# Two background streams of a mixer taken by turns, and its remaining rows loaded by six transfers

## The chip, the cores and the metric

One core of a Trainium2 chip runs the whole program in one launch. The metric is the device time of one execution in microseconds (us). The engines are named as in the profile: PE (TensorE matmuls), PEld (its weight loads), DVE (VectorE), ACT (ScalarE), POOL (GpSimd) and SP (SyncE, which issues most transfers).

## The reference, cut to what is computed

Three layers follow each other on 4 sequences of 576 rows and 512 columns.

```python
# attention, 8 heads of 64: keep the scores within tau of the row's maximum, softmax, times v
x = attn_out.transpose(0, 2, 1, 3).reshape(4, 576, 512)
# token-shift layer: x_prev is x moved by one row
k = np.maximum(xk @ w_k, 0.0); v = k * k @ w_v      # 512 -> 1024 -> 512
r = 1.0 / (1.0 + np.exp(-(xr @ w_r))); x = r * v
# mixer
X = np.fft.fft(np.fft.fft(x, axis=1), axis=2)
u = x + np.real(X)
un = (u - mean(u)) / np.sqrt(var(u) + 1e-6)
out = u + np.maximum(un @ w_ch1, 0.0) @ w_ch2       # 512 -> 2048 -> 512
```

## The kernel before

The program has two parts that overlap at their border. Attention and the token-shift layer (`ffn_stream`) fill the first 613 us. The mixer follows, and it is what the change touches.

**Products by halves.** A float32 matrix product is made of three products of rounded parts (high by high, high by low, low by high). So each weight has to be split into a high and a low part before use. `weight_pieces` (L46) does it in pieces of 256 columns: a load of 256 KB issued by ACT (L56), three DVE operations that put the raw bits together (L69 to L71), a copy on ACT (L75) and a subtraction (L79), which is on DVE for the first two quarters. The mixer's weights are prepared in four quarters; `quarter(q)` (L924) yields 16 times, once for each piece, first the eight of `w_ch1`, then the eight of `w_ch2`. The second quarter, `quarter(1)`, goes into tiles named cB.

**The transform.** The Fourier transform of one batch is made of matrix products with tables, after rows and columns were folded by symmetry. `fft_fold(b)` (L850) loads 256 pairs of rows (`load_pairs`, L753: four transfers of 256 KB) and the remaining rows (`load_rem`, L761), and folds them on DVE and ACT. `load_rem` fills two tiles of 98 rows, `ra` and `rb`: rows 0 to 31, 33 to 64 and 65 to 96 all hold the same 32 rows of the DRAM tensor `xd`, and rows 32 and 97 hold its row 576. That takes six transfers of 64 KB and four of 2 KB a batch, all from SP. `ra` and `rb` lie in the pool tag "o", which has four buffers in all; the tiles `un` of the normalisation (L977) and the last outputs `xnat` of the token-shift layer use the same four. `fft_one(b)` (L870) multiplies by the first tables (PE lines L802 to L805; L805 is the remaining rows' matmul) and `fft_two(b)` (L890) by the second (L817 to L828), and makes u. `fft_fold`, `fft_one` and `fft_two` yield 6, 3 and 2 times.

**The mixer's matmuls.** `mixer` (L1114) goes through pairs (quarter q, groups of 256 rows g). For each of four blocks f it issues `ch1` (L1088 to L1090, tile c1ps) of this pair and `ch2` (L1110 to L1112, tile c2ps) of the pair before. The first pairs are (0,0) to (0,3), then (1,0) to (1,3), then (0,4) and on. `norm(g)` (L975) loads the rows u of a group, normalises them and `turn(g)` (L998) transposes them on PE (L1005) and splits them (L1008 on ACT, L1009 on DVE) into the tile ut that `ch1` reads. `norm(2)` is asked for while (0,0) runs, for use in (0,2).

**The background.** What runs beside the mixer is a generator, `behind` (L1213): the second quarter's pieces, then the transforms of the third batch (b = 2) and the fourth (b = 3). In the first four pairs two steps of it are taken for each f. A scheduler then orders the instructions of every engine by when it expects them to be ready, with the order of the program as priority. So a step's place in the program is a priority, and not a place in time.

```python
behind = chain(
    quarter(1), fft_fold(2), fft_one(2), fft_two(2),
    fft_fold(3), fft_one(3), fft_two(3), fft_last(), done(),
)
```

Of the kernel before, what the change touches and what calls it, by code (L numbers as in the profile page):

```python
# [20 lines left out]
D, FF, FC = 512, 1024, 2048  # L21
# [8 lines left out]
def tile_kernel(ctx: ExitStack, tc: tile.TileContext, a):  # L30
    nc = tc.nc
    pe, dve, act, pool, sp = nc.tensor, nc.vector, nc.scalar, nc.gpsimd, nc.sync
# [5 lines left out]
    xd = [dram.tile([S + 1, D], F32, name=f"xd{b}") for b in range(B)]  # L38
# [45 lines left out]
    def whole(pair, base=0):  # L84
        return lambda c, n: [x[:, c - base:c - base + n] for x in pair]
# [6 lines left out]
    def big(slot, name):  # L92
        return wA.tile([128, 4096], F32R, tag=slot, name=name)

    def halves(p, name):
        return [wA.tile([128, 2048], F32R, tag=f"A{p}{i}", name=f"{name}{p}{i}") for i in range(2)]
# [40 lines left out]
    def settle():  # L137
        go, second[:] = list(second), []
        for f in go:
            f()  # L140
        while pending:
            pending.pop(0)()
# [610 lines left out]
    def load_pairs(b):  # L753
        xa = fp.tile([128, 2, D], F32, tag="xa", name="xa")
        xb = fp.tile([128, 2, D], F32, tag="xb", name="xb")
        for i in range(2):
            sp.dma_start(xa[:, i], xd[b][128 * i:128 * i + 128, :])
            sp.dma_start(xb[:, i], xd[b][288 + 128 * i:416 + 128 * i, :])
        return [(xa[:, i], xb[:, i]) for i in range(2)]

    def load_rem(b):  # L761

        xa = chp.tile([128, D], F32, tag="o", bufs=4, name="ra")[:98]
        xb = chp.tile([128, D], F32, tag="o", bufs=4, name="rb")[:98]
        for r in (0, 33, 65):
            sp.dma_start(xa[r:r + 32], xd[b][256:288, :])
            sp.dma_start(xb[r:r + 32], xd[b][544:576, :])
        for r in (32, 97):
            sp.dma_start(xa[r:r + 1], xd[b][576:577, :])
            sp.dma_start(xb[r:r + 1], xd[b][576:577, :])  # L770
        return xa, xb

    def folded(xa, xb, n):

        p, q, y = (fp.tile([128, 257], F32, tag="w", bufs=5, name=nm) for nm in ("fp", "fq", "fy"))
        act.activation(p[:n, 0:257:256], xa[:, 0:257:256], AF.Copy)
        act.activation(q[:n, 0:257:256], xb[:, 0:257:256], AF.Copy)
        dve.tensor_tensor(p[:n, 1:256], xa[:, 1:256], xb[:, 511:256:-1], op=ALU.add)
        dve.tensor_tensor(q[:n, 1:256], xb[:, 1:256], xa[:, 511:256:-1], op=ALU.add)
        dve.tensor_tensor(y[:n], p[:n], q[:n], op=ALU.add)  # L780
        dve.tensor_tensor(p[:n, 0:256], p[:n, 0:256], q[:n, 0:256], op=ALU.subtract)
        return y, p[:, 0:256]

    def split_tile(x, w, tag):
        hi = fp1.tile([128, w], F32R, tag=tag + "h", bufs=2, name=tag + "h")
        lo = fp1.tile([128, w], F32R, tag=tag + "l", bufs=2, name=tag + "l")
        act.activation(hi, x, AF.Copy)
        dve.tensor_tensor(lo, x, hi.bitcast(F32), op=ALU.subtract)
        return hi, lo

    def stack_tile(x, w, tag):
        st = fp1.tile([98, w], F32R, tag=tag, bufs=1, name=tag)
        act.activation(st, x[:98], AF.Copy)
        dve.tensor_tensor(st[0:33], x[0:33], st[0:33].bitcast(F32), op=ALU.subtract)
        return st
# [12 lines left out]
    def fsplit(hi, lo, ps):  # L808
        act.activation(hi, ps, AF.Copy)
        dve.tensor_tensor(lo, ps, hi.bitcast(F32), op=ALU.subtract)  # L810
# [39 lines left out]
    def fft_fold(b):  # L850
        while written[b] < 2:
            yield
        settle()
        prs = prs_of[b] = load_pairs(b)
        ra, rb = load_rem(b)
        parts_e, parts_o = [], []
        for xa, xb in prs:
            e, o = folded(xa, xb, 128)
            yield
            parts_e.append(split_tile(e, 257, "fse"))  # L860
            parts_o.append(split_tile(o, 256, "fso"))
            yield
        e, o = folded(ra, rb, 98)
        yield
        ske = stack_tile(e, 257, "ske")
        sko = stack_tile(o, 256, "sko")
        fold_of[b] = (parts_e, parts_o, ske, sko)
        yield

    def fft_one(b):  # L870
        parts_e, parts_o, ske, sko = fold_of.pop(b)
        G = [fp.tile([128, 2, 290], F32R, tag=f"G{i}", bufs=1, name=f"G{i}") for i in range(2)]
        Hh = [fp.tile([128, 2, HS], F32R, tag=f"H{i}", bufs=1, name=f"H{i}") for i in range(2)]
        for mc in range(2):
            o = stage_1(parts_e, ske, tc1, tc1r, 290, 128 * mc, 128 * mc + 128)
            fsplit(G[0][:, mc], G[1][:, mc], o)
            o = stage_1(parts_o, sko, ts1, ts1r, HS, 128 * mc, 128 * mc + 128)
            fsplit(Hh[0][:, mc], Hh[1][:, mc], o)
            yield
        o = stage_1(parts_e, ske, tc1, tc1r, 290, 256, 257)  # L880
        fsplit(g1[0:1], g1[32:33], o)
        sl = slice(32 * b, 32 * b + 32)
        act.activation(g1[64:65, sl], o[:, 256:288], AF.Copy)
        dve.tensor_tensor(g1[96:97, sl], o[:, 256:288], g1[0:1, 256:288].bitcast(F32), op=ALU.subtract)
        for i, x in enumerate((G[0], G[1], Hh[0], Hh[1])):
            act.activation(grem[i][:, :, b, :], x[:, :, 256:288].bitcast(F32), AF.Copy)
        spec[b] = (G, Hh)
        yield

    def fft_two(b):  # L890
        G, Hh = spec.pop(b)
        prs = prs_of.pop(b)
        z, _ = stage_2(G, None, 0, 288, 289)
        zr = fp.tile([1, 257], F32, name="zr")
        act.activation(zr, z[0:1, 0:257], AF.Copy)
        for i in range(2):
            pa, pb = stage_2(G, Hh, 0, 128 * i, 128 * i + 128)
            make_u(2 * b + i, pa, pb, *prs[i], z=zr if i == 0 else None)
            yield
# [12 lines left out]
    def chain(*gens):  # L912
        for g in gens:
            yield from g


    wq = {}
    SEVEN = (3,)
# [5 lines left out]
    def quarter(q):  # L924

        if q % 2:
            t = [big(f"B{i}", f"cB{i}") for i in range(2)]
            wq[q] = [[x[:, 2048 * k:2048 * k + 2048] for x in t] for k in range(2)]
        else:
            wq[q] = [halves(0, "cA"), None]  # L930
        todo = []
        for k, src in enumerate(("w_ch1", "w_ch2")):
            def to(c, n, k=k):
                if wq[q][k] is None:
                    wq[q][k] = halves(k, "cA")
                return whole(wq[q][k], 2048 * q)(c, n)

            todo += [(a[src], to, 8 * q + j) for j in ((0, 2, 4, 6, 1, 3, 5, 7) if k == 0 else range(8))]
        if q not in SEVEN:
            yield from weight_pieces(todo, None, stage2, 256, rb=3, bb=2, lows=dve if q < 2 else None)  # L940
            return
        more[q] = xwp.tile([128, 2, 3, 2, 256], F32R, name=f"more{q}")
        todo = todo[:8] + [(s, to if i % 4 != 1 else lambda c, n: None, 8 * q + i)
                           for (s, to, _), i in zip(todo[8:], (0, 1, 3, 2, 4, 5, 7, 6))]
        kept = {}

        def less(x, y, to):
            t = spare(F32)
            dve.tensor_tensor(t, x, y, op=ALU.subtract)
            act.activation(to[0], t, AF.Copy)  # L950
            pool.tensor_tensor(to[1], t, to[0].bitcast(F32), op=ALU.subtract)
            return t

        def then(k, wf):
            p, i = divmod(k - 8, 4)
            if k < 8:
                return
            ext = [[more[q][:, p, m, t] for t in range(2)] for m in range(3)]
            if i == 0:
                kept["b11"] = wf  # L960
            elif i == 1:
                kept["b12"] = wf
                kept["t1"] = less(wf, kept["b11"], whole(wq[q][1])(1024 * p + 256, 256))
            elif i == 2:
                less(wf, kept["b12"], ext[1])
                kept["t2"] = less(wf, kept["t1"], ext[0])
            else:
                less(wf, kept["t2"], ext[2])

        yield from weight_pieces(todo, None, stage2, 256, rb=3, bb=2, then=then)  # L970
# [240 lines left out]
    for _ in cgen:  # L1211
        pass
    behind = chain(  # L1213
        quarter(1), fft_fold(2), fft_one(2), fft_two(2),
        fft_fold(3), fft_one(3), fft_two(3), fft_last(), done(),
    )

# [2 lines left out]
    for (q, gs), f in mixer():  # L1220
        g = gs[-1]
# [142 lines left out]
```

## Time and profile before

| | us |
|---|---|
| median of three runs | 1053.23 |
| lowest and highest | 1051.57, 1055.49 |
| the profiled execution | 1055.04 |
| its span on the core | 1053.0 |
| PE busy in the span | 1003.0 |
| DVE, ACT, POOL busy | 717.3, 536.3, 395.4 |

The span is what the trace covers; some 2.0 us of the profiled execution lie around it. Times in the trace count from the span's start. "PE busy" is the share of time in which a matmul ran, and "PEclk" the clock that PE was granted, as a share of its full 2.4 GHz. A time behind an arrow is idle time of an engine just before an instruction, put down to what came last.

### The profile page before, as it was taken

How to read it: one execution, taken by the hardware profiler on the slowest of the kernel's cores; microseconds unless marked ns; L12 is line 12 of the kernel's file. 1: busy time of each engine (PE TensorE's matmuls, PEld its weight loads, DVE VectorE, ACT ScalarE, POOL GpSimd, SP SyncE). 2: the span in 40 equal slices, each digit the busy share in tenths (PEclk: the TensorE clock that was granted, in tenths of full speed). 3: DMA queues.
4: the chain of work that ended last, by engine and by line, in shares of the span. 5: the costliest groups of instructions: out<-in, count | busy, mean ns of one | idle time of the engine just before them, and what ended most of it. 6: DMA issues, size and time to landing. Idle time of an engine off the chain costs nothing.

```text
span 1053.0 us, 18827 instructions
## 1 busy us (share of the span) xinstructions
PE 1003.0 (95%) x6807; PEld 884.1 (84%) x6807; DVE 717.3 (68%) x1880; ACT 536.3 (51%) x1211; POOL 395.4 (38%) x495
## 2 busy tenths in 40 slices
PE   6887779999999999999999989999999999999998
PEld 4565659988889888999889879898998888889997
DVE  6799988667776685865356889457537449236776
ACT  4688777675866766857265745243313113113332
POOL 1445868465584564844233100000014125112231
PEclk9899989999999999999999989999999999999999
DMA  6442332121211212100613666536325335223221
GB/s 228 146 133 80 118 108 60 48 67 43 72 60 48 73 31 88 51 24 14 198 55 110 202 204 200 159 127 207 119 92 180 130 119 175 96 101 120 101 100 61
DMA packets 45636, 114.52 MB, mean 109 GB/s; under 512 B 6319, under 2 KB 6740, under 8 KB 45544
## 3 DMA queue, kind: packets, MB, share of 16 engines
q1 hardware_dynamic: 27920, 74.47, 22.2%
q10 hardware_dynamic: 12344, 22.13, 6.8%
q0 software_dynamic: 5280, 16.72, 4.4%
q8 instruction: 54, 0.88, 0.4%
q14 instruction: 38, 0.31, 0.1%
HBM read 84.98 MB, written 28.32 MB: 108 GB/s over the span
## 4 chain that ended last, share of the span: by engine, by line
PE 74%; DVE 10%; DMA 6%; ACT 3%; issue 3%; POOL 2%; SPq 0%; ACTq 0%; DVEq 0%; POOLq 0%
PE c1ps L1090 7%; PE c1ps L1089 6%; PE c1ps L1088 6%; PE s L227 5%; PE av L388 5%; PE c2ps L1112 5%; PE c2ps L1110 5%; PE c2ps L1111 5%; PE p L1045 4%; PE t L329 4%; PE kps L408 2%; PE kps L409 2%; PE kps L410 2%; DMA rawqk<-in_qk 2%; PE vps L530 2%
## 5 line engine op out<-in xcount | busy, mean ns | idle before, releaser
L267 DVE TENSOR_REDUCE small<-s 128x1 f32<-128x576 f32 x144 | 106.9, 752 | 48.1 <-PE s L227 37.3
L1159 POOL DMA_DIRECT2D ud<-u x54 | 29.5, 546 | 264.2 <-DVE u L1158 206.3
L290 POOL TENSOR_SCALAR e<-e,small 128x576 f32<-128x576 f32 x112 | 90.1, 811 | 87.9 <-DVE small L637 73.5
L282 DVE SCALAR_TENSOR_TENSOR e<-s,small,e 128x576 f32<-128x576 f32 x128 | 102.7, 812 | 25.6 <-ACT e L278 22.4
L278 ACT ACTIVATE e<-s,small 128x576 f32<-128x576 f32 x128 | 93.9, 745 | 31.1 <-DVE small L267 27.9
L1100 ACT ACTIVATE hh<-c1ps 128x256 fp32r<-128x256 f32 (+1 forms) x84 | 37.1, 443 | 137.2 <-PE c1ps L1090 111.6
L1101 DVE SCALAR_TENSOR_TENSOR hh<-c1ps,hh 128x256 fp32r<-128x256 f32 (+1 forms) x84 | 41.6, 496 | 89.2 <-ACT hh L1100 89.2
L329 PE MATMUL t<-ident,e 128*128 128x128 f32 x512 | 82.5, 278 | 12.9 <-ACT pt L332 6.5
L332 ACT ACTIVATE pt<-t 128x512 f32<-128x512 f32 x128 | 75.2, 599 | 22.3 <-PE t L329 20.6
L329 PEld LDWEIGHTS t<-ident,e 128*128 128x128 f32 x512 | 61.2, 142 | 24.3 <-issue 6.9
L488 POOL TENSOR_TENSOR k<-relu,k 128x288 fp32r<-128x288 f32 x64 | 54.3, 851 | 68.1 <-ACT k L486 63.9
L408 PE MATMUL kps<-xh,wk 128*128 128x288 f32 x256 | 78.1, 306 | 1.7 <-DVE tg L537 0.9
L530 PE MATMUL vps<-k,wv 128*128 128x288 f32 x256 | 77.5, 304 | 0.4 <-ACT tg L518 0.4
L531 PE MATMUL vps<-k,wv 128*128 128x288 f32 x256 | 77.3, 303 | 0.0
L532 PE MATMUL vps<-k,wv 128*128 128x288 f32 x256 | 76.7, 301 | 0.0
L410 PE MATMUL kps<-xh,wk 128*128 128x288 f32 x256 | 76.2, 298 | 0.0
L409 PE MATMUL kps<-xl,wk 128*128 128x288 f32 x256 | 76.2, 298 | 0.0
L1090 PE MATMUL c1ps<-ut,cB 128*128 128x256 f32 (+1 forms) x256 | 76.0, 297 | 0.0
L1089 PE MATMUL c1ps<-ut,cB 128*128 128x256 f32 (+1 forms) x256 | 75.8, 296 | 0.0
L1088 PE MATMUL c1ps<-ut,cB 128*128 128x256 f32 (+1 forms) x256 | 75.7, 296 | 0.0
L1088 PE MATMUL c1ps<-ut,cA 128*128 128x256 f32 (+1 forms) x224 | 71.0, 317 | 1.4 <-ACT ut L1008 1.4
L1089 PE MATMUL c1ps<-ut,cA 128*128 128x256 f32 (+1 forms) x224 | 70.7, 316 | 0.0
(270 smaller groups left out, 3116.4 us busy)
## 6 DMA issues: line engine op xcount, KB each, us to landing
u<-ud SPq DMA_DIRECT2D x36, 512.0 KB
wraw<-in_w_ch ACTq DMA_DIRECT2D x64, 256.0 KB
rawqk<-in_qk SPq DMA_DIRECT2D x24, 608.0 KB
ud<-u POOLq DMA_DIRECT2D x54, 256.0 KB, 2.5
v<-in_v SPq DMA_DIRECT2D x16, 320.0 KB
un<-ud SPq DMA_DIRECT2D x18, 256.0 KB
out<-u SPq DMA_DIRECT2D x18, 256.0 KB
wraw<-in_w_k SPq DMA_DIRECT2D x8, 512.0 KB
```

The costliest lines, as they stand in the source:

```text
L267: dve.tensor_reduce(st[:, 0:1], sps[n][:, :, 0:HS], axis=AX.XY, op=ALU.max, negate=True)
L278: act.activation(two(eview(n)), sps[n][:, :, 0:HS], AF.Exp, bias=st[:, 0:1])
L282: dve.scalar_tensor_tensor(e, sps[n][:, :, 0:HS], st[:, 1:2], e, op0=ALU.is_ge, op1=ALU.mult, accum_out=st[:, 2:3])
L290: pool.tensor_scalar(e, e, st[:, 2:3], 1.0, op0=ALU.mult, op1=ALU.mult)
L329: pe.transpose(t[:, k, :], e[:, o + 128 * k:o + 128 * (k + 1)], ident)
L408: pe.matmul(ps, wh, x[0][k], start=(k == 0), stop=False)
L409: pe.matmul(ps, wh, x[1][k], start=False, stop=False)
L410: pe.matmul(ps, wl, x[0][k], start=False, stop=(k == nk - 1))
L530: pe.matmul(ps, wv[0][:, c:c + 128], k2[0][:, k, :], start=(k == 0), stop=False)
L1088: pe.matmul(ps, wh, ut[0][:, k, :], start=(k == 0), stop=False)
L1089: pe.matmul(ps, wh, ut[1][:, k, :], start=False, stop=False)
L1090: pe.matmul(ps, wl, ut[0][:, k, :], start=False, stop=(k == 3))
```

## The change

Two edits. The remaining rows of a batch are loaded by six transfers where there were ten: for each of the two tiles one of 64 rows, which reads the 32 rows twice, one of 32 rows, and one that writes row 576 into rows 32 and 97. This holds for all four batches. And the second quarter's 16 pieces and the 11 steps of the third batch's transform alternate, one piece and one step, until one of the two is used up. The 27 steps take the same places in `behind` together; what follows them is where it was.

```diff
-        for r in (0, 33, 65):
-            sp.dma_start(xa[r:r + 32], xd[b][256:288, :])
-            sp.dma_start(xb[r:r + 32], xd[b][544:576, :])
-        for r in (32, 97):
-            sp.dma_start(xa[r:r + 1], xd[b][576:577, :])
-            sp.dma_start(xb[r:r + 1], xd[b][576:577, :])
+        for x, r in ((xa, 256), (xb, 544)):
+            rows = xd[b][r:r + 32, :]
+            sp.dma_start(x[33:97], rows.rearrange("(a p) d -> a p d", a=1).to_broadcast([2, 32, D]))
+            sp.dma_start(x[0:32], rows)
+            sp.dma_start(x[32:98:65], xd[b][576:577, :].to_broadcast([2, D]))
...
+    def by_turns(*gens):
+        left = list(gens)
+        while left:
+            for g in list(left):
+                try:
+                    next(g)
+                except StopIteration:
+                    left.remove(g)
+                    continue
+                yield
...
     behind = chain(
-        quarter(1), fft_fold(2), fft_one(2), fft_two(2),
+        by_turns(quarter(1), chain(fft_fold(2), fft_one(2), fft_two(2))),
         fft_fold(3), fft_one(3), fft_two(3), fft_last(), done(),
```

## Rows read from the trace of the kernel before

**Rows 1.** The page, part 2: PE busy in tenths of 40 slices.
```profile
PE   6887779999999999999999989999999999999998
```
**Rows 2.** Stretches: PE, PEld, DVE, ACT, POOL busy; PEclk, DMA share, GB/s.
```profile
600.00:650.00 50.00, 46.26 (x304) 42.87 (x305) 43.71 (x138) 23.57 (x58) 1.41 (x3) 0.93 0.66 211
650.00:700.00 50.00, 50.00 (x333) 44.99 (x332) 32.27 (x92) 16.70 (x51) 4.12 (x8) 1.00 0.48 153
```
**Rows 3.** PE's waits at the mixer's start: total, times, longest.
```profile
PE c1ps L1088 <- ACT ut L1008: 1.4, 1, 1.4
PE xn L548 <- DVE tg L537: 1.4, 1, 1.4
```
**Rows 4.** All waits of PE from 620 us to the end.
```profile
PE p L1045 <- DVE u L1051: 0.6, 1, 0.6
PE p L1045 <- ACT h L1027: 0.2, 1, 0.2
```
**Rows 5.** Timeline of PE, 613 to 621 us: start, length, instruction, idle before it.
```profile
615.13 0.76 PE L548 MATMUL xn<-ident,tg 128*128 128x128 f32 x5 [1.43 <-DVE tg L537]
...
618.20 0.58 PE L1088 MATMUL c1ps<-ut,cA 128*128 128x256 f32 x1 [1.45 <-ACT ut L1008]
619.20 1.97 PE L1005 MATMUL ut<-ident,un 128*128 128x128 f32 x8 [0.42 <-DVE ut L1009]
```
**Rows 6.** Stretches around the mixer's start; columns as in Rows 2.
```profile
616.00:620.00 4.00, 1.99 (x9) 1.40 (x10) 3.24 (x9) 2.95 (x7) 0.00 (x0) 0.63 0.97 293
620.00:624.00 4.00, 4.00 (x21) 4.00 (x20) 2.58 (x7) 1.64 (x4) 0.00 (x0) 0.51 1.00 370
```
**Rows 7.** Timeline of DVE, 600 to 640 us, around the mixer's start.
```profile
604.60 0.42 DVE L778 TENSOR_TENSOR fp<-xa,xb 128x255 f32<-128x255 f32 x1 [0.71 <-DMA xb<-xd]
...
613.28 0.76 DVE L70 SCALAR_TENSOR_TENSOR wbits<-wraw,wbits 128x256 int32<-128x256 int32 x2
613.95 0.76 DVE L71 SCALAR_TENSOR_TENSOR wbits<-wraw,wbits 128x256 int32<-128x256 int32 x2
614.62 0.45 DVE L537 SCALAR_TENSOR_TENSOR tg<-tg,vps 128x288 f32<-128x288 f32 x1
...
615.32 0.42 DVE L79 TENSOR_TENSOR cB<-wbits,cB 128x256 fp32r<-128x256 f32 x1
```
**Rows 8.** Tile ra: issues and readers; ns min/median/max, first and last start.
```profile
L766 SPq DMA_DIRECT2D ra<-xd x12: 302/414/487, 511.7 to 650.3; - x12
L769 SPq DMA_DIRECT2D ra<-xd x8: 215/256/302, 519.7 to 653.0; - x8
```
**Rows 9.** First batch's remainder: its last DVE operation, PE's first use.
```profile
533.19 0.41 DVE L794 TENSOR_TENSOR sko<-fp,sko 33x256 fp32r<-33x256 f32 x1
...
534.95 0.29 PE L805 MATMUL f<-tc1r,ske 98*128 98x290 f32 x1
```
**Rows 10.** A stretch in which the DMA engines are saturated; columns as in Rows 2.
```profile
600.00:605.00 5.00, 4.80 (x36) 4.80 (x37) 3.07 (x10) 1.87 (x8) 0.00 (x0) 1.00 0.96 325
```
**Rows 11.** Second quarter: the last piece's split on DVE, PE's first use of cB.
```profile
656.79 0.42 DVE L79 TENSOR_TENSOR cB<-wbits,cB 128x256 fp32r<-128x256 f32 x1
...
L1088 PE MATMUL c1ps<-ut,cB x256: 276/282/400, 671.5 to 1040.6; 128*128 128x256 f32 x112, 128*128 128x512 f32 x16
```
**Rows 12.** Third batch's first matmuls on PE: start of a group and its last.
```profile
656.42 0.29 PE L802 MATMUL f<-tc,fseh 128*128 128x290 f32 x1
...
657.22 0.30 PE L805 MATMUL f<-tc1r,ske 98*128 98x290 f32 x1
```
**Rows 13.** Timeline of SP's issues, 505 to 740 us: loads for norm and of ra.
```profile
620.25 6.62 SPq L979 DMA_DIRECT2D un<-ud  x4
639.07 1.25 SPq L766 DMA_DIRECT2D ra<-xd  x3
```
**Rows 14.** From norm(2)'s statistics on DVE to its use on PE (two timelines).
```profile
626.83 0.69 DVE L982 BATCH_NORM_STATS2 lnst<-un 128x6 f32<-128x512 f32 x1
...
640.90 0.28 PE L1088 MATMUL c1ps<-ut,cA 128*128 128x256 f32 x1
```

## The prediction

> **What bounds the kernel now.** I read the page's row of PE slices first: from slice 24 on, that is from about 620 us, PE is busy in nine tenths or more of every slice, and it is the only engine of which that holds [rows 1]. The stretches say it more exactly: 50.00 of 50 us from 650 to 700, at a granted clock of 1.00, but 46.26 of 50 from 600 to 650, at 0.93 [rows 2]. The list of PE's waits shows where these 3.74 us lie: a transpose that waited for the product tg on DVE, 1.4 us, and the mixer's first `ch1`, which waited for ut, 1.4 us [rows 3]. After 620 us PE waits twice, 0.8 us in all [rows 4]. So of what the change can reach, everything after 620 us is PE working, and the columns that PE has to stream are not changed by either edit. A gain can come only from the border at 613 to 624 us, or from before it.
>
> At the border, PE's timeline gives 1.43, 1.45 and 0.42 us of idle time, 3.3 us [rows 5]. Idle time costs a second time there, since the granted clock falls behind it: 0.63 from 616 to 620, 0.51 from 620 to 624, close to the lower of the two levels, 1.2 GHz [rows 6]. With PE's busy time in these two stretches that is 1.99 x 0.37 + 4.00 x 0.49 = 2.7 us. All that the border can give is therefore 6.0 us. A part of it is the order on DVE: the product tg, for which PE's transpose waits, starts at 614.62, behind four operations of weight pieces that began at 613.28, so 1.3 us [rows 7].
>
> **The change part by part.** The profiled execution took 1055.04 us, 1.8 us more than the median of the three runs; the sum is made on it and then lowered by 1.8.
>
> *Ten transfers become six.* SP spends a median of 414 ns on a transfer of 32 rows and 256 ns on one of a single row [rows 8]: 6 x 0.414 + 4 x 0.256 = 3.5 us a batch. With 0.414 for each of the new ones it is 2.5, so 1.0 us less on SP for each of four batches. SP isn't what PE waits for, so this is worth nothing by itself; what hides it is PE's other matmuls. What could be worth something is when the rows land. The first batch shows the tightest case: the remainder's last DVE operation ends at 533.60, PE takes it at 534.95 straight behind other matmuls [rows 9]. Earlier rows give nothing there, later ones cost all that goes beyond 1.35 us. Two things pull in opposite directions. The single-row transfers were first issued at 519.7, 8 us behind the first of 32 rows at 511.7 [rows 8]; six can be out sooner. But the copy of 64 rows is a form that the trace doesn't have. In a saturated stretch the 16 engines moved 325 GB/s at a share of 0.96 [rows 10], 21.2 GB/s for one engine. 64 rows of 2 KB, 131 KB, take 0.4 us on 16 engines and 6.2 us on a single one; for both tiles 0.8 to 12.4 us. The nearest row is that of the 32-row transfers, which are ordinary loads; I take the lower end, so a cost of 0, and keep the upper end for a rival.
>
> *Turns on DVE and ACT.* Piece n of the second quarter moves from step n to about step 2n, the last from step 16 to step 27. A piece is late by what the transform's steps put on DVE ahead of it. The pair folding has mostly gone already: it ran on DVE from 604.60, before the border, although its steps stood behind all 16 pieces [rows 7]. What remains are the 6 operations of the remaining rows, 6 of the first product's split and 12 that make u, some 24 of about 0.42 us: 10 us. The last piece's split began at 656.79, and PE first reads cB at 671.5 [rows 11]: 14.7 us of cover, which holds, and the pieces that are needed first come first. If the cover were gone, the price would be PE's wait for the piece, at most the excess over 14.7. Cost 0.
>
> *The third batch's matmuls move forward on PE.* One group of seven takes from 656.42 to about 657.35, 0.93 us [rows 12]. There are five such groups and 33 matmuls of the second stage, which I put at 0.13 each: 4.7 + 4.3 = 9 us. They are moved and not added: 0.
>
> *What is moved past on SP.* Before, the loads of `norm(2)` and `norm(3)` were issued from 620.25 and those of `ra` only at 639.07 [rows 13]. Now the transform's first step stands ahead of `norm(2)` in the program, and both want buffers of the tag "o". So `ra` and `rb` take the first free ones, and the loads of `norm(2)` wait in SP's queue behind six issues, 2.5 us. Its rows are due: the statistics begin at 626.83, and PE uses the result at 640.90, with nothing idle ahead [rows 14]. A delay of 2.5 us would be PE's, were it not that the third batch's remainder now comes 18.8 us earlier, so that its matmuls could start near 637.6 instead of 656.42, and 9 us of them can stand in. The cost lies between 0 and 2.5 us; I take 1.0, since PE's order is fixed beforehand and won't fit everywhere.
>
> *The border.* Which DVE operations stand ahead of tg and ut may change by a few: between a gain of 1.3 us and a loss of about the same. I take 0.
>
> Sum: 1055.04 + 1.0 - 1.8 = 1054.2 us.
>
> **The rivals.** *A, slower: the doubled copies crawl.* A copy that reads its source twice may be split over as many engines as there are repeats. On two engines each moves 32 rows of 2 KB for each tile, 65 KB at 21.2 GB/s: 3.1 us, 6.2 us for both [rows 10]. The place is the first batch's remainder: 6.2 less 1.35 is a wait of 4.8 us for PE at 534.95 [rows 9], and a wait of that size lowered the clock at the border, for 2.7 us more [rows 6]. 1053.2 + 7.5 = 1060.7 us. It decides once the rows land more than 1.35 us later than before. Against it: the six are issued earlier by several us, and the scheduler may put other matmuls ahead.
>
> The Trainium skill (DMA: Bandwidth & Descriptors, the sections "Why a DMA increments its semaphore by 16 and not by 1" and "Rules for kernel authors") says that a transfer runs on the largest number of engines, up to 16, that divides the outermost counts of both sides, so that a leading broadcast of two copies is confined to two engines. By this rule A's price would hold and the sum would be 1060.7; no run here shows it so far, as the trace has no such copy.
>
> *B, faster: the border closes.* If tg and ut no longer stand behind weight pieces, PE gets 1.3 us back, and with all of the border's 6.0 us the time would be 1047.2. For it: fewer pieces stand early in the program. Against it: the steps that replace them work on DVE too, tg has to wait for the last matmul in any case, and the first pieces are ready as before.
>
> *C, the change doesn't do what it says.* The order on DVE follows when things are ready: the third batch's fold was ahead of the border though it stood last [rows 7]. Then the turns change little but the remaining rows' place: 1053.2.
>
> **How the numbers follow.** The forecast, 1054.2, has 0.46, with a spread of 1050 to 1058; C 0.18; A 0.24; B 0.12, of which a third keeps only a part of the 6.0 us. What a measurement of this kernel can tell from no change is about 0.5%, 5.3 us. So faster by more than that: 0.09, from B; slower: 0.26, from A and the forecast's upper end; within: 0.65. The range leaves out B's full gain and A's worst, where a second wait at 640.90 adds to the first: 1048.5 to 1062.
>
> **What would show it.** Right: PE's stretches after 620 us stay at 50.00 of 50; the third batch's first matmuls stand before 650; the border's idle time is within 1.3 us of 3.3; SP issues six transfers for a batch. A is shown by an idle PE ahead of L805 near 535 and by long-lasting transfers of `ra`; B by a granted clock of 1.00 from 616 to 624; C by an unchanged place of the cB pieces. The forecast is wrong if PE waits for ut at (0,2) or for cB, or if the scheduler puts the stages before 510 us into another order, which nothing here prices.

## The result and the profile after

The change makes the kernel slower. The median is 1065.03 us where it was 1053.82 us (six runs of each). The ratio, here and below, is worked out from all runs and not from the two medians: 1.0112, with a 95% interval of 1.0085 to 1.0139 (below in square brackets). Each set of experiments was timed beside new runs of the kernel before, with medians of 1053.4 to 1054.3 us, and its ratios go by these. The prediction was 1054.2 us with a range up to 1062. The profiled execution took 1064.34 us, its span is 1062.4 us: 9.4 us more than the span before.

The page's row of PE slices, to be held against [rows 1]:

```profile
PE   6888889999999999999899888999999999999998
```

Slice 19 (505 to 531 us; the first is slice 0) and the three slices 22 to 24 (584 to 664 us) show an eight; in [rows 1] only slice 23 does. The stretches say how much is lost (columns as in [rows 2], to which the first two lines answer; the last two answer to [rows 6]). The third and the fourth line show one stretch, after and before:

```profile
600.00:650.00 50.00, 45.54 (x300) 41.32 (x298) 41.03 (x127) 22.45 (x56) 1.19 (x2) 0.97 0.68 215
650.00:700.00 50.00, 47.94 (x306) 43.49 (x305) 30.80 (x89) 16.88 (x48) 3.24 (x6) 0.93 0.45 150
524.00:532.00 8.00, 5.91 (x33) 5.55 (x31) 1.52 (x5) 2.74 (x9) 0.80 (x1) 0.79 0.24 84
524.00:532.00 8.00, 7.22 (x50) 6.36 (x49) 4.93 (x8) 5.81 (x17) 2.40 (x3) 1.00 0.55 153
616.00:620.00 4.00, 2.30 (x17) 1.52 (x15) 3.88 (x13) 2.65 (x6) 0.00 (x0) 1.00 0.72 220
620.00:624.00 4.00, 3.72 (x18) 3.67 (x19) 3.29 (x8) 2.49 (x6) 0.00 (x0) 0.57 1.00 309
```

Two places are new. From 524 to 532 us PE is idle for 2.1 of 8 us, where it was 0.8, and its clock is granted at 0.79, while the DMA engines are busy at a share of 0.24 only: something is waited for, and it isn't for want of DMA engines. And from 650 to 700 PE isn't full any more. PE's longest waits after 480 us, as a list (total, times, longest):

```profile
PE rps L408 <- ACT tg L518: 2.8, 2, 2.5
PE c1ps L1098 <- ACT ut L1018: 2.4, 2, 1.4
PE kps L408 <- ACT xnat L556: 2.1, 1, 2.1
PE f L801 <- DVE ut L1019: 2.1, 1, 2.1
PE c1ps L1098 <- DVE hh L1111: 1.5, 1, 1.5
```

None of these names a transfer of the remaining rows. One has to go one engine further back. Around the first batch's remainder, timelines of PE, ACT and DVE:

```profile
528.29 0.61 PE L408 MATMUL kps<-xh,wk 128*128 128x288 f32 x1 [2.09 <-ACT xnat L556]
...
527.54 0.21 ACT L775 ACTIVATE fp<-ra 98x2 f32<-98x2 f32 x1 [3.73 <-DMA ra<-xd]
527.65 0.58 ACT L556 ACTIVATE xnat<-xn 128x512 f32<-128x512 f32 x1
...
530.42 0.42 DVE L777 TENSOR_TENSOR fp<-ra,rb 98x255 f32<-98x255 f32 x1 [7.86 <-DMA rb<-xd]
```

ACT stood 3.73 us at the fold of the remaining rows until `ra` had landed. The copy `xnat` of another part of the program, for which PE waited, was the next instruction in ACT's queue. DVE stood 7.86 us for `rb` in the same way. The third batch shows the pattern again (ACT waits 2.52 us for `ra` and 2.46 us for `rb`), with SP in it; timelines of SP, ACT, DVE and PE (the issues of un answer to [rows 13], the statistics to [rows 14], the first group of the third batch's matmuls, L801, to [rows 12]):

```profile
621.62 0.62 SPq L767 DMA_DIRECT2D ra<-xd  x1
...
628.70 0.58 SPq L769 DMA_DIRECT2D rb<-xd  x1
629.40 5.70 SPq L989 DMA_DIRECT2D un<-ud  x4
...
629.49 0.21 ACT L775 ACTIVATE fp<-ra 98x2 f32<-98x2 f32 x1 [2.52 <-DMA ra<-xd]
...
634.53 0.69 DVE L992 BATCH_NORM_STATS2 lnst<-un 128x6 f32<-128x512 f32 x1
...
649.67 0.50 PE L1098 MATMUL c1ps<-ut,cA 128*128 128x256 f32 x2 [0.92 <-ACT ut L1018]
652.24 0.61 PE L801 MATMUL f<-tc,fseh 128*128 128x290 f32 x1 [2.06 <-DVE ut L1019]
```

The loads for `norm(2)` go out at 629.40 instead of 620.25, its statistics begin 7.7 us later, and `ch1` of (0,2) stands at 649.67 instead of 640.90.

### The profile page after: what moved, and what is told of

The parts are those of the page before. It is cut to its first block, busy times and chain, and to the rows that moved or that the text cites. A ratio compares the mean times of both kernels' runs of the same rounds, so it can differ in the third digit from the quotient of the medians.

```text
span 1062.4 us, 18790 instructions
## 1 busy us (share of the span) xinstructions
PE 1009.1 (95%) x6807; PEld 888.9 (84%) x6807; DVE 715.8 (67%) x1880; ACT 535.7 (50%) x1211; POOL 396.1 (37%) x495
## 4 chain that ended last, share of the span: by engine, by line
PE 70%; DVE 13%; DMA 8%; ACT 5%; issue 3%; POOL 2%; SPq 0%; ACTq 0%; DVEq 0%; POOLq 0%
PE c1ps L1100 6%; PE c1ps L1099 6%; PE c1ps L1098 6%; PE av L388 5%; PE s L227 5%; PE c2ps L1120 4%; PE c2ps L1122 4%; PE c2ps L1121 4%; PE p L1055 4%; PE t L329 4%; PE kps L408 2%; PE kps L409 2%; PE kps L410 2%; DMA rb<-xd 2%; PE vps L531 2%
```

## The experiments

**The theory after the result.** Two causes. The 64-row copy has an outermost count of 2, which is the first number of the pattern [2, 32, D] by which it reads; it lands late, since few DMA engines work on it, and ACT and DVE, which take their instructions in order, stand behind it. And the turns put `ra` and `rb` of the third batch ahead of the loads of `norm(2)` on SP. **Rivals:** the turns alone cost it, by their order; or six transfers make the scheduler find a worse order, and the copy is innocent.

### First set: each edit alone, and the copy spread wider

*Six transfers alone.* The edit of `load_rem` as in the change, the background in sequence as before.

> The six transfers alone, the second quarter and the third batch's transform in sequence as before. Theory (the doubled copy of 64 rows lands late, and the turns carry that to the mixer's second-next normalisation): in the changed kernel PE lost some 5 us between 510 and 604 us, around the first batch's remainder, and some 9 us between 626 and 660 us, where ra and rb stand ahead of the loads of norm(2). Without the turns only the first loss should stay: 1053.8 + 5 = 1059, a ratio of 1.003 to 1.007, with ra and rb of the first batch landing near 527 to 530 us and PE working without a wait from 626 to 660. Rival 1 (the turns by themselves cost it all, transfers are hidden): 1052 to 1055, ratio 1.000. Rival 2 (a smaller number of transfers changes the order that the scheduler makes of the whole, and that order is worse): 1064, ratio 1.010.

Measured: 1064.87 us, ratio 1.0111 [1.0091, 1.0130]. So the whole loss comes without the turns, too, which neither my theory nor rival 1 had expected; the size is that of rival 2.

*Turns alone.* `by_turns` as in the change, ten transfers.

> The turns alone, the remaining rows by ten transfers as before. Theory: ra and rb still stand ahead of the loads of norm(2) on SP, but 32-row transfers land within some 2 us, so norm(2) is late by the ten issues only, 3.5 us against a slack that the trace of before doesn't show: 1053 to 1057, ratio 0.999 to 1.003. Rival 1 (the turns cost it all): PE loses the same 9 us between 626 and 660: 1062, ratio 1.008 or more.

Measured: 1060.32 us, ratio 1.0066 [1.0046, 1.0085]. The turns cost much more than I gave them. SP's timeline and the stretches (columns as in [rows 2]) show where:

```profile
620.30 0.32 SPq L766 DMA_DIRECT2D ra<-xd  x1
...
627.34 0.25 SPq L770 DMA_DIRECT2D rb<-xd  x1
627.91 5.07 SPq L990 DMA_DIRECT2D un<-ud  x4
```

```profile
640.00:650.00 10.00, 7.14 (x40) 5.44 (x38) 9.26 (x31) 4.66 (x9) 1.08 (x2) 0.98 0.84 263
650.00:660.00 10.00, 10.00 (x63) 9.32 (x62) 7.74 (x29) 4.62 (x11) 0.00 (x0) 0.84 0.61 187
```

The ten issues take not 3.5 but 7.3 us, from 620.30 to 627.59, with pauses between them. The loads of un are 7.66 us later than in [rows 13], and PE loses 2.86 us between 640 and 650 and, at a clock of 0.84, another 1.6 us of work in the ten behind. These 4.5 us are two thirds of the 6.9 us that the run lost; the rest was not placed.

*Both edits, the copy by row pairs.* Each row twice in a row, so that the outermost count is 32, and the table's rows in the same order:

```diff
-            sp.dma_start(x[33:97], rows.rearrange("(a p) d -> a p d", a=1).to_broadcast([2, 32, D]))
+            sp.dma_start(x[33:97], rows.rearrange("p (a d) -> p a d", a=1).to_broadcast([32, 2, D]))
...
-        return np.concatenate([hi, last, hi, lo, last], 0)
+        return np.concatenate([hi, last, np.stack([hi, lo], 1).reshape(64, -1), last], 0)
```

> The changed kernel with one thing different: the 64-row copy reads each of its 32 rows twice in a row (row pairs) where it read the block of 32 twice, so that its outermost count is 32 and not 2; the table's rows for the remainder are put in the same order. Every engine has its instructions in the same order as in the changed kernel. Theory: the copy then spreads over all engines and lands within 1 to 2 us; both losses go (5 us around 530, most of the 9 us from 626 to 660): 1050 to 1055, ratio 0.997 to 1.002, 2-KB packets on many queues' engines at once. Rival 1 (the turns and their order cost it): 1062 to 1066, the same as the changed kernel, with ra early.

Measured: 1056.90 us, ratio 1.0031 [1.0020, 1.0042]. With the instructions of every engine in the same order, 8.5 of the change's 11.8 us go. What is left is more than I expected.

*Six transfers alone, by row pairs.* The same copy, the background in sequence.

> The six transfers alone, with the 64-row copy reading each row twice in a row as in the run before. Theory: no loss around 530 us, so 1051 to 1054.5, ratio 0.997 to 1.001. Rival 2 (the order that the scheduler makes with six transfers is worse by itself): the same as the six transfers alone with the block read twice.

Measured: 1053.83 us, ratio 1.0010 [0.9998, 1.0021]. Against 1.0111 with the block read twice (in the two traces the instructions of PE, ACT, DVE and POOL stand in the same order), this settles rival 2: the order that comes with six transfers costs nothing that can be told from zero, and the copy's form alone costs 0.0101, 10.6 us.

### Second set: the two places of the copy, and the place of the loads

*Turns alone, the third batch's rows asked for later.*

```diff
-        ra, rb = load_rem(b)
+        if b != 2:
+            ra, rb = load_rem(b)
...
+        if b == 2:
+            ra, rb = load_rem(b)
         e, o = folded(ra, rb, 98)
```

> The turns alone (ten transfers), with one thing different for the third batch: its remaining rows are loaded at the step that folds them, not at the first step of the transform. Theory: what costs the 6.9 us of the turns alone is that ten issues of ra and rb stand ahead of the loads of norm(2) on SP (620.30 to 627.59, the loads of un then at 627.91 where they were at 620.25). With the rows asked for later, norm(2) is first again and its loads go out near 620: 1053 to 1056, ratio 0.999 to 1.003, PE without a wait of over 0.5 us between 640 and 650. Rival (the transform's steps on DVE and ACT ahead of norm(2) cost it): 1058 to 1061, ratio 1.005 or more, with un's loads early all the same.

Measured: 1054.86 us, ratio 1.0008 [0.9996, 1.0019]. SP's first issue for `norm(2)`:

```profile
619.30 0.83 SPq L993 DMA_DIRECT2D un<-ud  x2
620.26 3.85 SPq L766 DMA_DIRECT2D ra<-xd  x3
```

With norm(2)'s loads first again, the turns cost nothing that can be told from zero. So it was the place on SP, and not the steps on DVE and ACT.

*The block read twice in one batch only*, the others by row pairs; first in the first batch, then in the third:

```diff
+            if b == 0:
+                sp.dma_start(x[33:97], rows.rearrange("(a p) d -> a p d", a=1).to_broadcast([2, 32, D]))
+            else:
+                sp.dma_start(x[33:97], rows.rearrange("p (a d) -> p a d", a=1).to_broadcast([32, 2, D]))
```

> The six transfers alone with the rows read in pairs, but in the first batch the 64-row copy reads the block of 32 rows twice, as the change does. (In this batch the rows then lie in another order than the table's, so this batch's remainder is summed with the wrong rows of the table; the work is the same.) Every engine has its instructions in the same order. Theory: the first batch's copy alone costs PE's delay around 528 us that the two runs with this order show (6.2 us between instructions of the same place at 525 and 531, of which some 1.5 are given back by 600): 1058 to 1060.5, ratio 1.004 to 1.007. Rival (the copy costs only in the third batch, the first one's delay is made good later): 1053 to 1055.

> The same with the third batch's copy alone reading the block of 32 rows twice. (This batch's remainder is summed with the wrong rows of the table.) Theory: the third batch's copy costs the delay that the two runs of this order show between 640 and 659 us, 5.3 us: 1058 to 1060, ratio 1.004 to 1.006. The two parts then add to about the 11 us of the six transfers alone, and the second and fourth batch cost nothing. Rival (the third batch's delay comes only on top of a mixer that is late already): 1053 to 1055.

Measured: 1059.06 us, ratio 1.0042 [1.0028, 1.0056], for the first batch, and 1058.48 us, 1.0042 [1.0027, 1.0057], for the third. Each costs 0.0032 over the version with pairs, 3.4 us. Together that is 6.7 of the 10.6 us.

*Both causes taken away*: row pairs, turns, and the third batch's rows at the step that folds them.

> Six transfers with the rows read in pairs, the turns, and the third batch's remaining rows loaded at the step that folds them. Theory: with both causes taken away nothing is left of the loss: 1051 to 1055, ratio 0.998 to 1.001, against 1056.9 with the rows loaded at the first step. Rival (the steps taken by turns cost what is left): 1056 to 1058.

Measured: 1052.32 us, ratio 0.9982 [0.9970, 0.9995]: faster than the kernel before, by 1.9 us, though the interval only just leaves out 1. Against the row pairs in sequence (1.0010) the turns so bring 3.0 us, which with ten transfers they did not (1.0008); where this gain comes from was not separated. One stretch, first of the change and then of this version, shows that PE is full again:

```profile
640.00:660.00 20.00, 16.91 (x92) 14.90 (x92) 16.76 (x57) 8.62 (x21) 2.27 (x4) 0.83 0.62 202
640.00:660.00 20.00, 20.00 (x136) 18.57 (x135) 16.82 (x53) 9.36 (x24) 1.08 (x2) 1.00 0.78 228
```

### Third set: is it the outermost count?

*A block of 16 rows read four times, and one of 8 rows read eight times*, in place of 32 rows read twice:

```diff
-            sp.dma_start(x[33:97], rows.rearrange("(a p) d -> a p d", a=1).to_broadcast([2, 32, D]))
+            sp.dma_start(x[33:97], rows[0:16].rearrange("(a p) d -> a p d", a=1).to_broadcast([4, 16, D]))
```

> The six transfers alone, in sequence, with the 64-row copy reading a block of 16 rows four times, where the change reads 32 rows twice: the same bytes and the same 2-KB rows, an outermost count of 4. (Rows 16 to 31 of the remainder are so left out of the low parts' products.) Every engine has its instructions in the same order as in the six transfers alone. Theory (the copy is confined to as many DMA engines as its outermost count): the rows land in about half the time, and more than half of the 11.4 us goes, as a part of the delay lies under cover: 1054 to 1059, ratio 1.001 to 1.005. Rival (reading the same rows again is slow in itself, however they are spread): 1063 to 1067, ratio 1.010 or more, no better than two copies.

> The same with a block of 8 rows read eight times, an outermost count of 8. (Rows 8 to 31 of the remainder are so left out of the low parts' products.) Theory: nearly as good as the rows read in pairs, 1053 to 1056, ratio 0.999 to 1.002. Rival: as slow as two copies or slower, 1063 or more.

Measured: 1056.72 us, ratio 1.0028 [1.0017, 1.0040], with four and 1053.15 us, 0.9994 [0.9983, 1.0006], with eight. The summary of tile ra tells how long ACT sat idle ahead of its reading until `ra` had landed (us in all, times). In this order for two, four and eight repeats and for the row pairs:

```profile
  DMA ra<-xd: 9.9, 2
```

```profile
  DMA ra<-xd: 4.6, 2
```

```profile
  DMA ra<-xd: 2.8, 1
```

```profile
  DMA ra<-xd: 2.5, 1
```

| outermost count | ACT's wait for ra, us | ratio |
|---|---|---|
| 2 | 9.9 | 1.0111 |
| 4 | 4.6 | 1.0028 |
| 8 | 2.8 | 0.9994 |
| 32 (row pairs) | 2.5 | 1.0010 |

All four have the same bytes and the same instructions in the same order. From two to four the wait halves. The sum mixes two batches: in the first the wait falls from 3.85 to 0.80 us and is gone with eight and with the pairs; in the third it falls from 6.04 to 3.78, and the 2.84 and 2.48 us that stay there with eight and with the pairs don't show in the ratio. The transfers say it more directly: the last of the first batch's rows of 2 KB was moved 19.3, 17.4, 14.5 and 12.2 us after `ra` was issued, with two, four, eight and 32. Reading the same rows more often isn't slow in itself, or four and eight would be no better than two.

*The change with the third batch's rows asked for later*, the copy as the change has it.

> The changed kernel with the third batch's remaining rows loaded at the step that folds them, and the 64-row copy as the change has it (the block of 32 rows read twice). Every engine has its instructions in the same order as in the version without both causes (1052.3). Theory: the place in SP's queue is mended and the copy isn't, so the first batch's 4.4 us and most of the third's 4.5 us stay, on 1052.3: 1057 to 1062, ratio 1.004 to 1.008. Rival (behind norm(2) the copy is covered in the third batch, too, and in the first the delay was the turns'): 1052 to 1055.

Measured: 1062.30 us, ratio 1.0085 [1.0066, 1.0104], just above what the theory expected. The place alone mended gives back 2.8 us (1.0112 to 1.0085, which the two intervals don't tell from nothing), the copy alone 8.5 us (1.0112 to 1.0031), both 13.7 us (to 0.9982).

*The block read twice in the first and third batch together* (`if b in (0, 2)`).

> The six transfers alone with the rows read in pairs, and the block read twice in the first and third batch together (in these two the remainder is summed with the wrong rows of the table). Every engine has its instructions in the same order. What is open: by ratios the first batch's copy alone costs 0.0032 and the third's alone 0.0032 over the version with pairs (1.0010), 0.0064 together, but all four copies cost 0.0101. Theory (the second batch's copy keeps alive the first one's delay, which PE makes good by 3 us near 590 us when the second batch's rows are in time): first and third add, ratio 1.006 to 1.0085, 1060 to 1063. Rival (the first and the third delay make each other worse, the second and fourth batch do nothing): ratio 1.010 to 1.012, 1064.5 to 1066.5.

Measured: 1061.51 us, ratio 1.0073 [1.0057, 1.0089]. So first and third add: 0.0063 over the pairs. The remaining 0.0038, 4.0 us, comes with the second and the fourth batch. My reason for it, though, isn't what the traces show. Set beside each other instruction by instruction, the profiled executions of the row pairs and of all four batches doubled differ by 3.3 us at 515 us (times of the row pairs' execution), by 9.0 at 536, 7.8 at 604 to 640, 11.3 at 653 and 13.2 from 659 on; with the first and third doubled the differences are 2.0, 6.0, 3.8, 7.4 and 7.3. The step of 1.9 us between 653 and 659 is there only when the fourth batch is doubled, whose `ra` is issued at 655.52 of its own time; about 1 us can be the second batch's (between 536 and 604 us PE makes good 1.2 us in the one and 2.2 in the other), and the first batch's own step is 1.7 us larger in the one profile than in the other, with the same copy in both, which stays open. That the fourth batch's copy holds up a weight piece's load there (DVE waits 1.76 us for it, and 0.37 us with the first and third doubled) was not tried by itself.

### All of it in one table

Ratios to the kernel before:

| remaining rows | in sequence | by turns | by turns, third batch's rows late |
|---|---|---|---|
| ten transfers | 1 | 1.0066 | 1.0008 |
| six, block read twice | 1.0111 | 1.0112 | 1.0085 |
| six, row pairs | 1.0010 | 1.0031 | 0.9982 |

The first row's middle and the second row's first cell are the two edits alone. They don't add (1.0177). The last column suggests why: the place of norm(2)'s loads (middle less last) costs 6.1, 2.8 and 5.2 us in the three rows, and the turns with the place mended (last less first) cost 0.8 us with ten transfers, which is not clear of zero, but gain 2.7 and 3.0 us with six. In the second row cost and gain would cancel. This isn't shown, as there each of the two is within the noise of its runs.

## Why the prediction was wrong

**The step that failed** is the cost of *ten transfers become six*. It bounded the copy from both sides, 0.8 to 12.4 us, and then took the lower end because "the nearest row is that of the 32-row transfers, which are ordinary loads". Nearest in bytes it was; but what decides, by the series of 2, 4, 8 and 32, is the outermost count, and by that it isn't near them at all. Cost taken: 0. Measured: 10.6 us (1.0111 against 1.0010).

**Rival A had the mechanism**, and its chance of 0.24 was too small. In the trace of the change, SP's queue moves 39 rows of 2 KB from 528 to 530 us, 84 ns each: 39 x 84 ns is 3.3 us of engine time in 2 us, which is 1.6 engines at work. By the rule of the Trainium skill (DMA: Bandwidth & Descriptors, "Rules for kernel authors") a leading broadcast of two copies goes over at most two; these rows and the series of two, four and eight agree. But its price for one batch, 7.5 us, was too high (3.4 us by ratio, though PE's delay at that place was 4.0 to 5.7 us in the three traces of this order with the first batch's block read twice, of which 1.2 to 2.2 us was made good by 604), and its place was too narrow. PE waited 0.5 us at the remainder's matmul itself (532.60), and 2.1 us ahead of that for `xnat`, behind ACT's wait. And the third batch pays as much as the first, the fourth and second another 4.0 us together. The prediction had left "A's worst, where a second wait at 640.90 adds to the first", out of the range: that is what came.

**SP's order**: right in kind, too small in size. The prediction named the tag and the queue, priced six issues at 2.5 us, and took 1.0. Put back in its place it returns 6.1 us with ten transfers (1.0066 less 1.0008) and 5.2 us with six by row pairs (1.0031 less 0.9982); as the turns there gain 3.0 us themselves, only 2.2 of these show against the same copy in sequence (1.0010). Two things were missed. The issues don't follow each other at 0.4 us: SP pauses between them, so un came 7.66 us later in the one case and 5.6 in the other (625.82 instead of 620.25). And the cover that I named, the third batch's matmuls which could "stand in", wasn't used: PE's order is fixed beforehand, and it waited at (0,2). In the change itself the term doesn't show, 1.0112 against 1.0111: by the table the turns' own gain may make up for it, which isn't shown.

**What held.** *The turns on DVE and ACT* cost nothing (1.0008 with the loads in place, 0.9982 with six transfers by row pairs). The last piece's split stood at 662.39 and PE first read cB at 683.5, 21 us of cover. *Fewer transfers* are worth nothing by themselves (1.0010). *The border* stayed in sum about where it was: its idle time fell from the 3.3 us of [rows 5] to 1.7 (0.28 and 1.45, the third wait is gone). The clock of 1.00 from 616 to 620, where [rows 6] has 0.63, isn't rival B's sign, which asked for 1.00 up to 624: the mixer's first `ch1` stands 2.1 us later (620.28 for 618.20), and the clock falls behind it, to 0.57 from 620 to 624. With PE's 3.72 us there that costs 1.6 us, where the prediction had 2.7. The wait of 2.5 us for tg at 598.33, at the head of the list above, took about as much back. This wait, 2.2 to 2.5 us long, stands in all the versions with six transfers, also in the one with 1.0010. *The columns PE streams* didn't change.

**Of the signs named**, an idle PE ahead of the first remainder (526 to 533, where 535 was named) and late rows of `ra` were there, and told A. PE's wait for ut at (0,2), named as a sign that the forecast is wrong, came too (0.92 us at 649.67). The third batch's matmuls didn't come before 650 (652.24); with both causes gone they do (642.55).

## What to carry to other kernels

Ask of every transfer that you merge what its outermost count becomes; a repeat belongs on the inside, each row twice, and not the block twice. And when a load moves forward in the program, look at what stands behind it on its issuing queue, and behind its readers on theirs: the price here was paid by work that had nothing to do with the remaining rows.

## What the runs showed of the hardware

The copy with an outermost count of 2 landed much later among other traffic than its bytes say. An estimate of what it takes alone, if it goes over two engines: 32 rows of 84 ns for each, 2.7 us a tile. In the first batch of the change `ra` was issued at 510.01, its reader was released at 527.54, and SP's queue moved the last row of `ra` and `rb` at 529.62. Not all of this is the copy's own: the four loads of 256 KB by `load_pairs` went out on SP just ahead of it, and ACT waited for the last of them until 519.48. With the wide copy, issued at 510.00, the last row was moved at 522.20. So 7.4 us are the narrow copy's. From 520 to 526 us SP's queue moved only 11 to 40 rows of 2 KB in each 2 us, at 98 to 141 ns, while POOL's queue moved pieces of some 4 KB at 178 to 246 ns, 16 to 122 of them in each 2 us. How much of the delay this sharing makes was not tried.

On SP the wide copy by pairs costs as much as the narrow one, 0.60 against 0.62 us, and more than a transfer of 32 rows (0.414 in [rows 8]); SP's time told nothing of when the rows landed.
